# Reading the moving columns of every float32r matmul from two halves in turns

## The chip, the core and the metric

The kernel runs on one NeuronCore of a Trainium2 chip. A core has a matrix engine (TensorE, in the profile PE, its weight loads PEld), three engines for element-wise work (VectorE or DVE, ScalarE or ACT, GpSimd or POOL), a queue engine (SyncE or SP) and DMA engines. Operands lie in the on-chip memory SBUF, 128 partitions wide; matmuls write to the accumulators in PSUM, from which VectorE and ScalarE copy. The metric is the device time of one execution in microseconds.

## The reference

```python
# q, k, v: (4, 6080, 256); moe_w_in: (256, 2048); moe_w_out: (2048, 256)
qn = q / (np.linalg.norm(q, axis=1, keepdims=True) + 1e-06)
kn = k / (np.linalg.norm(k, axis=1, keepdims=True) + 1e-06)
s = kn.transpose(0, 2, 1) @ qn / tau          # 4 x 256 x 256
a = softmax(s, axis=-1)
x = (v @ a).reshape(24320, 256)
h = x @ w_in                                   # 24320 x 2048
g = np.where(h > 0.0, h, np.exp(np.minimum(h, 0.0)) - 1.0)
out = g @ w_out                                # 24320 x 256
```

The softmax is written in one word here; the reference subtracts the maximum and adds 1e-9 to the sum. The weights arrive as 64-bit floats and are converted on the chip.

## The kernel before

Attention is over channels, so for one batch a is a matrix of 256 x 256. The kernel multiplies it into the first weight matrix once per batch (wp = a times w_in, 256 x 2048), and what is left for each token is h = v wp, the ELU, and g w_out. Tokens are the columns: v comes in and the output goes out with channels first. The 24320 tokens are cut into 48 chunks, twelve per batch, eight of 512 and four of 496 columns (`chunk_sizes`). The 2048 hidden channels are cut into 16 tiles of 128, and one step (c, f) is one chunk and one such tile, 768 in all.

Nearly all products are in float32r, and each number of an operand is split into two float32r parts, hi and lo (`split`: ScalarE rounds to hi, VectorE subtracts). A product takes three matmuls: hi by hi, lo by hi, hi by lo. In a step `h_item` issues six into a PSUM tile ph (two contraction tiles of three, lines L323 to L325, moving operand vt, weights wp); `elu` makes e out of ph; `split_g` makes the pair g out of e; and three steps later (LAG = 3) `out_item` issues six into two PSUM tiles po (two output tiles of three, L361, L363, L365, moving operand g, weights wo). At a chunk's last step `store` copies the two po tiles to SBUF (L387) and sends them out. There are three po buffers and two are in use by a chunk.

In all of these the moving operand is a run of consecutive columns, such as `g[:, x, 0:n]`, 4 bytes a column, and each matmul writes its result's columns in the order in which it reads the moving ones. Two more kinds of float32r product run beside the steps: `gram_item` builds q-k products of the next batch from rows that were split in `split_rows` (L166 with 512 columns, in two runs of 256, and L169 with 256), and `wp_item` builds wp of the next batch (L283 to L285), scaled by the softmax's sums on its way out of PSUM (L289, L290). `softmax` reads the gram tiles (L229, L230). Batch 0 uses plain float32 for its gram (L446), its transposes and its wp (L281). Their moving operands are consecutive too.

The order of the engines' instructions is the program's order: a table of side jobs by step (`at`, `loose`, `fine`) sets where a conversion, a load or a gram matmul is issued among the steps.

After the last store twelve matmuls write a PSUM tile pd that nothing reads, the idle products: three plain ones (L696), three whose moving operand is one column repeated n times (L698), three on the same bytes seen as bf16 (L700), three on 64 of the 128 rows (L702).

Of the kernel before, what the change touches and what calls it, by code (L numbers as in the profile page):

```python
# [7 lines left out]
F32 = mybir.dt.float32  # L8
F32R = mybir.dt.float32r
U32 = mybir.dt.uint32  # L10
BF16 = mybir.dt.bfloat16
AF = mybir.ActivationFunctionType
ALU = mybir.AluOpType
AX = mybir.AxisListType
# [6 lines left out]
def chunk_sizes(n, most):  # L21

    unit = 16 if n % 16 == 0 else 2
    count = -(-n // most)
    low, more = divmod(n // unit, count)
    return [unit * (low + (x < more)) for x in range(count)]


@with_exitstack
def channel_attention_then_elu_ffn(ctx: ExitStack, tc, q, k, vT, tau, w_in, w_out, outT):  # L30
# [8 lines left out]
    nc = tc.nc  # L39
    B, N, C = q.shape  # L40
# [3 lines left out]
    P = 128  # L44
    KT = C // P
    FT = F // P
    DT = D // P
    CH = 512
    sizes = chunk_sizes(N, CH)
    NB = len(sizes)  # L50
    NCH = B * NB
# [7 lines left out]
    WB = 3  # L59
# [9 lines left out]
    ps = ctx.enter_context(tc.tile_pool(name="ps", bufs=4, space=bass.MemoryType.PSUM))  # L69
# [9 lines left out]
    wo = const.tile([P, FT, 2, D], F32R, name="wo")  # L79
# [78 lines left out]
    def gram_item(hl, gram, ct, first, last):  # L158

        pg = gram[ct]
        cs = slice(ct * P, ct * P + P)
        for r in range(2):
            yield nc.tensor.matmul(  # L166
                pg, hl[:, 0, 1, r, cs], hl[:, :, 0, r, :], start=(first and r == 0), stop=False
            )
            yield nc.tensor.matmul(  # L169
                pg[:, 0, :], hl[:, 1, 1, r, cs], hl[:, 0, 0, r, :], start=False, stop=(last and r == 1)  # L170
            )

    def keep_warm(n):
# [43 lines left out]
    def softmax(b, gram, pn, rk, nm):  # L217

        a = work.tile([P, KT, C], F32, tag="a", bufs=1, name=f"a_{b}")
        sm = tiny.tile([P, KT], F32, tag="sums", bufs=2, name="sums")
        for ct in range(KT):
            r = rk[:, ct : ct + 1]
            if b == 0:
                nc.vector.tensor_scalar(a[:, ct], gram[ct][:, 0, :], r, None, op0=ALU.mult)
                continue
            nc.scalar.copy(a[:, ct], gram[ct][:, 1, :])  # L229
            nc.vector.tensor_add(a[:, ct], gram[ct][:, 0, :], a[:, ct])  # L230
            if b == 1:
                nc.vector.tensor_add(a[:, ct], a[:, ct], early[:, ct])
            nc.vector.tensor_scalar(a[:, ct], a[:, ct], r, None, op0=ALU.mult)
        for ct in range(KT):
            nc.vector.tensor_mul(a[:, ct], a[:, ct], pn[:, 1, :])
            nc.vector.tensor_reduce(nm[:, ct : ct + 1], a[:, ct], axis=AX.X, op=ALU.max, negate=True)
            nc.scalar.activation(
                a[:, ct], a[:, ct], AF.Exp, bias=nm[:, ct : ct + 1], accum_out=sm[:, ct : ct + 1]
            )
        nc.vector.tensor_scalar(sm, sm, 1e-9, None, op0=ALU.add)  # L240
        done = nc.vector.reciprocal(sm, sm)
        return a, sm, done.ins
# [31 lines left out]
    def wp_item(aT, rs, wi, wp, ct, fq, part=0, parts=1):  # L274
        n = CH // parts
        pw = ps.tile([P, CH], F32, tag="w", bufs=WB, name="pw")[:, 0:n]
        cs = slice(ct * P, ct * P + P)
        ws = slice(part * n, part * n + n)
        for jt in range(KT):
            if wi.dtype == F32:  # L280
                nc.tensor.matmul(pw, aT[:, jt, cs], wi[:, jt, ws], start=(jt == 0), stop=(jt == KT - 1))  # L281
                continue
            nc.tensor.matmul(pw, aT[:, 0, jt, cs], wi[:, 0, jt, ws], start=(jt == 0), stop=False)  # L283
            nc.tensor.matmul(pw, aT[:, 0, jt, cs], wi[:, 1, jt, ws], start=False, stop=False)  # L284
            nc.tensor.matmul(pw, aT[:, 1, jt, cs], wi[:, 0, jt, ws], start=False, stop=(jt == KT - 1))  # L285
        f0 = fq * CH + part * n
        hi, lo = (wp[ct][:, x, f0 : f0 + n] for x in range(2))
        r = rs[:, ct : ct + 1]
        nc.scalar.activation(hi, pw, AF.Copy, scale=r)  # L289
        nc.vector.scalar_tensor_tensor(lo, pw, r, hi.bitcast(F32), op0=ALU.mult, op1=ALU.subtract)  # L290


    def span(c):

        b, x = divmod(c, NB)
        return b, b * N + sum(sizes[:x]), sizes[x]
# [17 lines left out]
    wps = {}  # L314

    def h_item(c, f, vt):
        b, _, n = span(c)
        wp = wps[b]
        ph = ps.tile([P, CH], F32, tag="w", bufs=WB, name="ph")
        fs = slice(f * P, f * P + P)  # L320
        for kt in range(KT):
            hi, lo = (vt[:, kt, x, 0:n] for x in range(2))
            nc.tensor.matmul(ph[:, 0:n], wp[kt][:, 0, fs], hi, start=(kt == 0), stop=False)  # L323
            nc.tensor.matmul(ph[:, 0:n], wp[kt][:, 0, fs], lo, start=False, stop=False)  # L324
            nc.tensor.matmul(ph[:, 0:n], wp[kt][:, 1, fs], hi, start=False, stop=(kt == KT - 1))  # L325
        return ph
# [22 lines left out]
    def first(c, f):  # L349
        return f == 0 or (c, f) in [(x, lo) for x, lo, _ in pieces]  # L350

    def last(c, f):
        return f == FT - 1 or (c, f) in [(x, hi - 1) for x, _, hi in pieces]

    def out_item(c, f, g, po, between):

        n = span(c)[2]
        hi, lo = (g[:, x, 0:n] for x in range(2))
        for dt in range(DT):
            o, ds = po[dt][:, 0:n], slice(dt * P, dt * P + P)  # L360
            nc.tensor.matmul(o, wo[:, f, 0, ds], hi, start=first(c, f), stop=False)  # L361
            next(between, None)
            nc.tensor.matmul(o, wo[:, f, 1, ds], hi, start=False, stop=False)  # L363
            next(between, None)
            nc.tensor.matmul(o, wo[:, f, 0, ds], lo, start=False, stop=last(c, f))  # L365
            next(between, None)

    def store(c, f, po):
        _, t0, n = span(c)
        ov = outT[:, t0 : t0 + n].rearrange("(k p) t -> p k t", p=P)  # L370
        if c < M:
            o = half[c]
        else:
            o = work.tile([P, DT, CH], F32, tag="o", bufs=1, name="o")
        for dt in range(DT):
            if c < M and (c, 0, f + 1) not in pieces:
                nc.vector.tensor_add(o[:, dt, 0:n], o[:, dt, 0:n], po[dt][:, 0:n])
            elif c == NCH - 1 and dt == DT - 1:

                m = n // 2  # L380
                nc.vector.tensor_copy(o[:, dt, 0:m], po[dt][:, 0:m])
                nc.scalar.copy(o[:, dt, m:n], po[dt][:, m:n])
                nc.sync.dma_start(ov[:, dt, 0:m], o[:, dt, 0:m])
                nc.scalar.dma_start(ov[:, dt, m:n], o[:, dt, m:n])
                continue
            else:
                nc.scalar.copy(o[:, dt, 0:n], po[dt][:, 0:n])  # L387
            if f == FT - 1:
                nc.sync.dma_start(ov[:, dt], o[:, dt, 0:n])

# [50 lines left out]
    wi64, wo64, vraw, vts = {}, {}, {}, {}  # L441
# [8 lines left out]
    with tc.manual_schedule(engines={nc.tensor.engine, nc.sync.engine}):  # L450
# [95 lines left out]
        for part in range(2):  # L546
            for ct in range(KT):
                wp_item(aT0, rs0, wf[0], wps[0], ct, 0, part, 2)
# [49 lines left out]
    for c in range(NCH - 1):  # L598
# [6 lines left out]
        x, y = ((1, 2), (4, 6), (17, 19))[c] if c < M - 1 else (c * FT + 9, c * FT + 12)  # L605
# [6 lines left out]
    for b in range(1, B):  # L612
# [18 lines left out]
        def gram(b, g, ct):  # L631
            g0 = first_group(b)
            yield from gram_item(state[b, "hl", g], state[b, "gram"], ct, g == g0, g == NG - 1)
# [10 lines left out]
        for g in range(g0, NG):  # L644
            x = s0 + length * (g - g0) // (NG - g0)
# [5 lines left out]
        x = s1 - FT - 6  # L651
# [12 lines left out]
    for i in range(len(steps) + LAG):  # L664
        if i < len(steps):
            c, f = steps[i]
# [5 lines left out]
        if j >= 0:  # L672
            c, f = steps[j]
# [12 lines left out]
                fn()  # L686

    c, n = NCH - 1, span(NCH - 1)[2]
    pd = ps.tile([P, CH], F32, tag="w", bufs=WB, name="pd")
    hi, lo = (vts[c][:, 0, x, 0:n] for x in range(2))
    wide, narrow = wps[B - 1][0][:, 0, 0:P], wo[:, 0, 0, 0:P]
    for _ in range(3):
        nc.tensor.matmul(pd[:, 0:n], wide, hi, start=True, stop=True)  # L696
    for w in (narrow, wide, narrow):
        nc.tensor.matmul(pd[:, 0:n], w, vts[c][:, 0, 0, 0:1].to_broadcast([P, n]), start=True, stop=True)  # L698
    for w, m in ((wide, hi), (narrow, lo), (wide, hi)):
        nc.tensor.matmul(pd[:, 0:n], w.bitcast(BF16)[:, 0:P], m.bitcast(BF16)[:, 0:n], start=True, stop=True)  # L700
    for w, m in ((wide, hi), (narrow, lo), (wide, hi)):
        nc.tensor.matmul(pd[:, 0:n], w[0 : P // 2], m[0 : P // 2], start=True, stop=True)  # L702


# [1 line left out]
_INS = ["q", "k", "v", "tau", "moe_w_in", "moe_w_out"]  # L706
_OUTS = [((256, 24320), "float32")]
# [26 lines left out]
```

## Time and profile before

| | us |
|---|---|
| median of 3 runs | 2292.24 |
| lowest and highest run | 2290.45, 2293.08 |
| the profiled execution | 2289.16 |
| its span, first to last instruction | 2287.4 |

| engine | busy us | share of the span | instructions |
|---|---|---|---|
| TensorE, matmuls | 2283.2 | 100% | 10244 |
| TensorE, weight loads | 1900.3 | 83% | 10244 |
| VectorE | 1533.4 | 67% | 2395 |
| ScalarE | 1480.7 | 65% | 2425 |

The granted TensorE clock is 1.000 over the whole span. A matmul's duration in the records reaches from its start to the modelled end of its last column and overlaps the next matmul; the distance from one start to the next is read from the timeline, where a row has the start in us, the duration in us, the engine, the line, the operation, output and inputs, and the shape. A row of a group has the line, engine, operation, output and inputs, shape and count, then the busy time in us and the mean in ns, then the engine's idle time before it. A row of waits has who waited for whom, the total in us, how many times, and the longest.

### The profile page before, as it was taken

The page shows a single profiled execution, that of the slowest core. Times are in us where ns is not written, and L with a number is a line of the kernel's source. Part 1 is how long each engine was busy: PE and PEld are TensorE (multiplying, and loading weights), DVE is VectorE, ACT ScalarE, POOL GpSimd, SP SyncE. Part 2 cuts the span into 40 slices and gives each one's busy share as a digit, 9 for nine tenths or more (in the row PEclk, how much of TensorE's full clock was granted, in tenths as well). Part 3 has the DMA queues.
Part 4 walks back from the last instruction along what each step waited for, and adds up shares of the span by engine and source line. Part 5 has one row for each costly group of instructions (what it writes and reads, how often), then busy time and mean ns, then how long its engine had stood idle before and what let it go on. Part 6 is the DMA issues. An engine that isn't in the chain of part 4 may idle for free.

```text
span 2287.4 us, 27142 instructions
## 1 busy us (share of the span) xinstructions
PE 2283.2 (100%) x10244; PEld 1900.3 (83%) x10244; DVE 1533.4 (67%) x2395; ACT 1480.7 (65%) x2425; POOL 3.2 (0%) x11
## 2 busy tenths in 40 slices
PE   9999999999999999999999999999999999999999
PEld 8778888888888888888888888888888888888888
DVE  6995766666666666666666667666666666666665
ACT  5876666666666666666666666666666666666665
POOL 0000000000000000000000000000000000000000
DMA  9220111110201111111111111121102000000000
GB/s 356 83 74 19 61 59 65 55 53 37 65 28 56 47 53 49 55 55 44 37 55 37 46 47 56 47 64 46 47 34 64 20 19 28 28 19 10 19 9 19
DMA packets 61092, 118.15 MB, mean 52 GB/s; under 512 B 6048, under 2 KB 15904, under 8 KB 60960
## 3 DMA queue, kind: packets, MB, share of 16 engines
q1 hardware_dynamic: 60816, 116.29, 15.0%
q8 instruction: 80, 1.31, 0.2%
q14 instruction: 52, 0.43, 0.1%
q10 hardware_dynamic: 144, 0.13, 0.0%
HBM read 89.39 MB, written 27.00 MB: 51 GB/s over the span
## 4 chain that ended last, share of the span: by engine, by line
PE 97%; DMA 1%; DVE 1%; ACT 0%; issue 0%; SPq 0%; DVEq 0%; ACTq 0%
PE ph L323 15%; PE po L365 15%; PE po L361 15%; PE po L363 15%; PE ph L325 15%; PE ph L324 15%; PE gram L166 3%; PE gram L169 1%; DMA room<-in_k_dram 1%; PE pw L281 1%; PE pw L284 0%; PE pw L285 0%; PE pw L283 0%; DVE acc L145 0%; DMA wi<-in_moe_w_in_dram 0%; DMA raw<-in_k_dram 0%
## 5 line engine op out<-in xcount | busy, mean ns | idle before, releaser
L82 ACT CAST g<-e 128x512 fp32r<-128x512 f32 (+1 forms) x768 | 472.4, 615 | 507.6 <-DVE e L340 275.2
L83 DVE TENSOR_TENSOR g<-e,g 128x512 fp32r<-128x512 f32 (+1 forms) x768 | 526.4, 685 | 349.4 <-ACT g L82 314.1
L361 PE MATMUL po<-g,wo 128*128 128x512 f32 (+1 forms) x1536 | 596.0, 388 | 0.3 <-ACT g L82 0.3
L365 PE MATMUL po<-g,wo 128*128 128x512 f32 (+1 forms) x1536 | 596.0, 388 | 0.0
L363 PE MATMUL po<-g,wo 128*128 128x512 f32 (+1 forms) x1536 | 595.4, 388 | 0.0
L323 PE MATMUL ph<-vt,wp 128*128 128x512 f32 (+1 forms) x1472 | 573.6, 390 | 0.0
L325 PE MATMUL ph<-vt,wp 128*128 128x512 f32 (+1 forms) x1472 | 570.7, 388 | 0.0
L324 PE MATMUL ph<-vt,wp 128*128 128x512 f32 (+1 forms) x1472 | 569.6, 387 | 0.0
L336 DVE SCALAR_TENSOR_TENSOR e<-e,ph 128x512 f32<-128x512 f32 (+1 forms) x416 | 283.6, 682 | 297.2 <-ACT e L335 296.4
L334 ACT ACTIVATE e<-ph 128x512 f32<-128x512 f32 (+1 forms) x416 | 247.1, 594 | 159.2 <-PE ph L325 155.7
L361 PEld LDWEIGHTS po<-g,wo 128*128 128x128 f32 x1536 | 288.4, 188 | 58.3 <-ACT g L82 0.7
L363 PEld LDWEIGHTS po<-g,wo 128*128 128x128 f32 x1536 | 288.4, 188 | 57.7
L365 PEld LDWEIGHTS po<-g,wo 128*128 128x128 f32 x1536 | 288.3, 188 | 52.3 <-DVE g L83 0.4
L323 PEld LDWEIGHTS ph<-vt,wp 128*128 128x128 f32 x1472 | 276.2, 188 | 56.6 <-PE po L365 0.6
L325 PEld LDWEIGHTS ph<-vt,wp 128*128 128x128 f32 x1472 | 276.3, 188 | 56.3
L324 PEld LDWEIGHTS ph<-vt,wp 128*128 128x128 f32 x1472 | 276.4, 188 | 56.0 <-issue 0.7
L335 ACT ACTIVATE e<-e 128x512 f32<-128x512 f32 (+1 forms) x416 | 261.2, 628 | 12.1
L338 ACT ACTIVATE e<-ph 128x512 f32<-128x512 f32 (+1 forms) x352 | 208.7, 593 | 79.2 <-PE ph L325 64.7
L340 DVE TENSOR_TENSOR e<-ph,e 128x512 f32<-128x512 f32 (+1 forms) x352 | 241.1, 685 | 10.7
L339 DVE TENSOR_SCALAR e<-e 128x512 f32<-128x512 f32 (+1 forms) x352 | 148.9, 423 | 49.7 <-ACT e L338 49.6
L145 DVE TENSOR_TENSOR acc<-acc,sq 128x1024 f32<-128x1024 f32 x84 | 102.6, 1221 | 12.1 <-ACT sq L144 11.4
L166 PE MATMUL gram<-qk 128*128 128x512 f32 x276 | 108.5, 393 | 0.0
(126 smaller groups left out, 1173.4 us busy)
## 6 DMA issues: line engine op xcount, KB each, us to landing
raw<-in_q_dram SPq DMA_DIRECT2D x73, 256.0 KB, 2.7
raw<-in_k_dram SPq DMA_DIRECT2D x73, 256.0 KB, 2.9
v<-in_v_dram SPq DMA_DIRECT2D x32, 512.0 KB, 3.4
out_dram<-o SPq DMA_DIRECT2D x56, 256.0 KB, 2.0
v<-in_v_dram SPq DMA_DIRECT2D x16, 496.0 KB, 3.5
out_dram<-o SPq DMA_DIRECT2D x31, 248.0 KB, 2.1
wraw<-w_scr SPq DMA_DIRECT2D x12, 512.0 KB, 3.1
room<-in_q_dram SPq DMA_DIRECT2D x16, 256.0 KB, 5.2
```

Of the source, the lines that this page charges most:

```text
L82: nc.scalar.copy(hi, src)
L83: nc.vector.tensor_sub(lo, src, hi.bitcast(F32))
L323: nc.tensor.matmul(ph[:, 0:n], wp[kt][:, 0, fs], hi, start=(kt == 0), stop=False)
L324: nc.tensor.matmul(ph[:, 0:n], wp[kt][:, 0, fs], lo, start=False, stop=False)
L325: nc.tensor.matmul(ph[:, 0:n], wp[kt][:, 1, fs], hi, start=False, stop=(kt == KT - 1))
L334: nc.scalar.activation(ev, pv, AF.Relu, scale=-1.0)
L335: x = nc.scalar.activation(ev, ev, AF.Exp, scale=-1.0)
L336: y = nc.vector.scalar_tensor_tensor(ev, ev, -1.0, pv, op0=ALU.add, op1=ALU.max)
L340: y = nc.vector.tensor_tensor(ev, pv, ev, op=ALU.max)
L361: nc.tensor.matmul(o, wo[:, f, 0, ds], hi, start=first(c, f), stop=False)
L363: nc.tensor.matmul(o, wo[:, f, 1, ds], hi, start=False, stop=False)
L365: nc.tensor.matmul(o, wo[:, f, 0, ds], lo, start=False, stop=last(c, f))
```

## The change

Four helpers give views of a run of columns. `in_turns` lists column 0, column n/2, column 1, column n/2 + 1 and so on. The others are used where a result is taken out of PSUM, so that its columns come back into their own order: `halves` with `halves_of_turns` after one product in turns, `quarters` with `quarters_of_turns` after two (the columns of ph, e and g are in turns after the first product, and g is read in turns again).

All float32r matmuls read their moving operand through `in_turns`. Number and order of the matmuls and their weights stay as they are. The element-wise work between ph and g is unchanged, in the changed column order. The idle products are left out.

```diff
+def in_turns(cols):
+    if len(cols.shape) == 3:
+        return cols.rearrange("p x (a b) -> p x b a", a=2)
+    return cols.rearrange("p (a b) -> p b a", a=2)
+
+def halves(cols):
+    return cols.rearrange("p (a b) -> p a b", a=2)
+
+def halves_of_turns(cols):
+    return cols.rearrange("p (b a) -> p a b", a=2)
+
+def quarters(cols):
+    return cols.rearrange("p (r s q) -> p r s q", r=2, s=2)
+
+def quarters_of_turns(cols):
+    return cols.rearrange("p (q r s) -> p r s q", r=2, s=2)
...
 # gram_item
-                pg, hl[:, 0, 1, r, cs], hl[:, :, 0, r, :], start=(first and r == 0), stop=False
+                pg,
+                hl[:, 0, 1, r, cs],
+                in_turns(hl[:, :, 0, r, :]),
...
-                pg[:, 0, :], hl[:, 1, 1, r, cs], hl[:, 0, 0, r, :], start=False, stop=(last and r == 1)
+                pg[:, 0, :],
+                hl[:, 1, 1, r, cs],
+                in_turns(hl[:, 0, 0, r, :]),
...
 # softmax
-            nc.scalar.copy(a[:, ct], gram[ct][:, 1, :])
-            nc.vector.tensor_add(a[:, ct], gram[ct][:, 0, :], a[:, ct])
+            row = halves(a[:, ct])
+            nc.scalar.copy(row, halves_of_turns(gram[ct][:, 1, :]))
+            nc.vector.tensor_add(row, halves_of_turns(gram[ct][:, 0, :]), row)
...
 # wp_item
-            nc.tensor.matmul(pw, aT[:, 0, jt, cs], wi[:, 0, jt, ws], start=(jt == 0), stop=False)
-            nc.tensor.matmul(pw, aT[:, 0, jt, cs], wi[:, 1, jt, ws], start=False, stop=False)
-            nc.tensor.matmul(pw, aT[:, 1, jt, cs], wi[:, 0, jt, ws], start=False, stop=(jt == KT - 1))
+            whi, wlo = (in_turns(wi[:, x, jt, ws]) for x in range(2))
+            nc.tensor.matmul(pw, aT[:, 0, jt, cs], whi, start=(jt == 0), stop=False)
+            nc.tensor.matmul(pw, aT[:, 0, jt, cs], wlo, start=False, stop=False)
+            nc.tensor.matmul(pw, aT[:, 1, jt, cs], whi, start=False, stop=(jt == KT - 1))
...
+        if wi.dtype != F32:
+            hi, lo, pw = halves(hi), halves(lo), halves_of_turns(pw)
...
 # h_item
-            hi, lo = (vt[:, kt, x, 0:n] for x in range(2))
+            hi, lo = (in_turns(vt[:, kt, x, 0:n]) for x in range(2))
...
 # out_item
-        hi, lo = (g[:, x, 0:n] for x in range(2))
+        hi, lo = (in_turns(g[:, x, 0:n]) for x in range(2))
...
 # store
+            y, x = quarters(o[:, dt, 0:n]), quarters_of_turns(po[dt][:, 0:n])
             if c < M and (c, 0, f + 1) not in pieces:
-                nc.vector.tensor_add(o[:, dt, 0:n], o[:, dt, 0:n], po[dt][:, 0:n])
+                nc.vector.tensor_add(y, y, x)
...
-                nc.vector.tensor_copy(o[:, dt, 0:m], po[dt][:, 0:m])
-                nc.scalar.copy(o[:, dt, m:n], po[dt][:, m:n])
+                nc.vector.tensor_copy(y[:, 0], x[:, 0])
+                nc.scalar.copy(y[:, 1], x[:, 1])
...
-                nc.scalar.copy(o[:, dt, 0:n], po[dt][:, 0:n])
+                nc.scalar.copy(y, x)
...
-    pd = ps.tile([P, CH], F32, tag="w", bufs=WB, name="pd")
...
-        nc.tensor.matmul(pd[:, 0:n], w[0 : P // 2], m[0 : P // 2], start=True, stop=True)
```

More of the change, by code (lines that the diff above doesn't have):

```diff
@@ L10 @@
 U32 = mybir.dt.uint32
-BF16 = mybir.dt.bfloat16
 AF = mybir.ActivationFunctionType
@@ L166, in gram_item @@
             yield nc.tensor.matmul(
-                pg, hl[:, 0, 1, r, cs], hl[:, :, 0, r, :], start=(first and r == 0), stop=False
+                pg,
+                hl[:, 0, 1, r, cs],
+                in_turns(hl[:, :, 0, r, :]),
+                start=(first and r == 0),
+                stop=False,
             )
             yield nc.tensor.matmul(
-                pg[:, 0, :], hl[:, 1, 1, r, cs], hl[:, 0, 0, r, :], start=False, stop=(last and r == 1)
+                pg[:, 0, :],
+                hl[:, 1, 1, r, cs],
+                in_turns(hl[:, 0, 0, r, :]),
+                start=False,
+                stop=(last and r == 1),
             )
@@ L686, in channel_attention_then_elu_ffn @@
                 fn()
-    c, n = NCH - 1, span(NCH - 1)[2]
-    pd = ps.tile([P, CH], F32, tag="w", bufs=WB, name="pd")
[L693 to L702, printed above, removed]
 _INS = ["q", "k", "v", "tau", "moe_w_in", "moe_w_out"]
```

## The prediction

> **What bounds the kernel now.** I read the page's first part, then the chain that ended last, then what TensorE waited for.
>
> ```profile
> span 2287.4 us, 27142 instructions
> PE 2283.2 (100%) x10244; PEld 1900.3 (83%) x10244; DVE 1533.4 (67%) x2395; ACT 1480.7 (65%) x2425; POOL 3.2 (0%) x11
> PE 97%; DMA 1%; DVE 1%; ACT 0%; issue 0%; SPq 0%; DVEq 0%; ACTq 0%
> ```
>
> ```profile
> PE pd L177 <- DVE ones L78: 1.1, 1, 1.1
> ...
> PE po L361 <- ACT g L82: 0.3, 1, 0.3
> ```
>
> TensorE is on 97% of the chain. The list of its waits has five entries; the largest and the last are shown, 1.1 us and 0.3 us, so nothing else holds it up worth the name. The other two engines stand a third idle. The time is therefore the number of matmuls times the distance from one start to the next, and a busy share can't tell that distance, since the 0.39 us of one matmul overlap the following one. So I counted in the groups of instructions, kept apart by form, and read distances from the timeline.
>
> ```profile
> L365 PE MATMUL po<-g,wo 128*128 128x512 f32 x1024 | 399.8, 391 | 0.0
> L323 PE MATMUL ph<-vt,wp 128*128 128x512 f32 x960 | 376.5, 392 | 0.0
> L323 PE MATMUL ph<-vt,wp 128*128 128x496 f32 x512 | 197.1, 385 | 0.0
> L166 PE MATMUL gram<-qk 128*128 128x512 f32 x276 | 108.5, 393 | 0.0
> L169 PE MATMUL gram<-qk 128*128 128x256 f32 x276 | 76.7, 278 | 0.0
> L323 PE MATMUL ph<-scr_r,wp 128*128 128x512 f32 x64 | 26.2, 409 | 0.0
> L285 PE MATMUL pw<-wi,aT 128*128 128x512 f32 x48 | 18.7, 390 | 0.0
> ```
>
> Six lines (L323, L324, L325, L361, L363, L365) carry 1024 matmuls of 512 columns each (960 + 64 for the first three) and 512 of 496. With 276 at L166 and 48 at each of L283 to L285 that makes 6144 + 276 + 144 = 6564 float32r matmuls of 512 columns, 3072 of 496 and 276 of 256.
>
> ```profile
> 169.01 0.39 PE L323 MATMUL ph<-vt,wp 128*128 128x512 f32 x1
> ...
> 177.17 0.39 PE L323 MATMUL ph<-vt,wp 128*128 128x512 f32 x1
> ```
>
> ```profile
> 2278.22 0.38 PE L361 MATMUL po<-g,wo 128*128 128x496 f32 x1
> ...
> 2283.28 0.38 PE L365 MATMUL po<-g,wo 128*128 128x496 f32 x1
> ```
>
> ```profile
> 814.49 0.28 PE L169 MATMUL gram<-qk 128*128 128x256 f32 x1
> 814.60 0.40 PE L365 MATMUL po<-g,wo 128*128 128x512 f32 x1
> ```
>
> Between the first two rows lie 36 steps: 8.16 / 36 = 0.2267 us for 512 columns. Between the next two lie 23: 5.06 / 23 = 0.2200 us for 496. The 256 columns take 0.11 us. The first two are 0.443 ns a column, and the third agrees within its last digit, so the distance goes with the columns and has next to no fixed part: 6564 x 0.2267 + 3072 x 0.2200 + 276 x 0.11 = 2194 us of the 2287.4.
>
> **The change, part by part.** The matmuls, their weights and their order stay. Only the order in which the moving columns are read differs: column j, then column j + n/2, which lies n x 2 bytes on (1 KB at 512). No row of this trace has such a read, so its price is bounded. What the trace has is one set of reads that are cheaper than consecutive ones, and one that takes twice as long.
>
> ```profile
> 2284.16 0.37 PE L698 MATMUL pd<-vt,wo 128*128 128x496 f32 x1
> ...
> 2284.80 0.38 PE L700 MATMUL pd<-vt,wp 128*128 128x496 bf16 x1
> ...
> 2285.23 0.37 PE L700 MATMUL pd<-vt,wp 128*128 128x496 bf16 x1
> ```
>
> ```profile
> 57.26 3.45 PE pw L281 x16
> 92.03 1.72 PE pw L281 x4
> ```
>
> L698 reads one column over and over: three starts in 0.64 us, 0.2133 each, against 0.2200 for 496 different columns. L700 reads half as many bytes: two in 0.43 us, 0.215. The weights at L698 are loaded as float32, as for any other matmul. So what makes 0.2200 out of 0.213 is the fetching of moving columns: at 4 bytes a column the read path is already the slower party, by 3%, with the easiest addresses there are. The second fence, from the chain in order of time, is the plain float32 product: 1.72 / 4 = 0.430 us for 512 columns and 3.45 / 16 = 0.2156 for 256, both at half the column rate.
>
> Lower end of the price: the new order removes the 3%. Upper end: every distance doubles, because two consecutive columns no longer come out of neighbouring addresses and each needs a fetch of its own. I take the second kind, at the distance of the nearest row in which the array takes a column every other beat, 0.430 us. The reason is the row before: a path that falls behind with neighbouring addresses has nothing to spare for scattered ones. The terms:
> - 512 columns: 6564 x (0.430 - 0.2267) = 1334 us
> - 496 columns: 3072 x (0.430 x 496/512 - 0.2200) = 604 us
> - 256 columns: 276 x (0.2156 - 0.11) = 29 us
>
> Together +1967 us. With doubled distances instead it would be the 2194 us themselves.
>
> The Trainium skill bears on this in Advanced Engine Details and Errata, section SBUF Cachelines: the memory is read in lines of 16 bytes, at least two hits on a line are needed to absorb its latency, and a different line on every access is penalised. It gives no price. Here consecutive reading has four float32 columns on a line, reading in turns has one, so by that rule the time goes up, and by the measured distances alone (order of addresses free) it would stay at 2292; no run so far shows a read of one column per line.
>
> The order of the columns is undone in four places, which costs the other engines something. wp is written through a column view (24 pairs at L289 and L290, one for every six of the 144), a softmax row likewise (6 pairs), and the output copy reads PSUM with a step of four columns and writes quarters.
>
> ```profile
> L335 ACT ACTIVATE e<-e 128x512 f32<-128x512 f32 x288 | 182.1, 633 | 8.3
> ...
> L95 ACT ACTIVATE cv<-wi 128x512 f32<-128x512 f32 x8 | 5.4, 673 | 0.7 <-DVE wf L107 0.6
> ```
>
> ```profile
> 2244.76 1.23 ACT L387 COPY o<-po 128x496 f32<-128x496 f32 x2
> ...
> 2247.20 0.38 PE L361 MATMUL po<-g,wo 128*128 128x496 f32 x1
> ```
>
> L95 reads every second word and takes 673 ns against 633 for a consecutive read of that size: 40 ns dearer. That, or at most as much again as the copy itself (0.6 us), is the price of one output copy. By the loops there are 95 (48 chunks of two, less the last half chunk) and 14 additions at L377. The cover is a chunk's end: two copies run from 2244.76 to 2245.99, and of the three po buffers the one freed first is wanted again at 2247.20. Behind the copies on ScalarE stands the next rounding of g, whose product comes two steps (5 us) later. Doubled copies would end at 2247.2 for both, the first at 2246.0, still in time. I put all four places at nothing; with slower matmuls the cover grows. Without cover it would be 95 x 0.6 = 57 us.
>
> The idle products at the end stand beside the last stores:
>
> ```profile
> 2284.55 0.38 ACTq L384 DMA_DIRECT2D out_dram<-o  x1
> ...
> 2286.08 0.39 PE L702 MATMUL pd<-vt,wp 64*128 64x496 f32 x1
> ```
>
> ```profile
> out_dram<-o ACTq DMA_DIRECT2D x1, 124.0 KB, 1.8
> ```
>
> The last store lands at 2284.55 + 1.8 = 2286.4, the last idle product ends at 2286.5. Taking them away gains 0.1 us, and the strided reads of the two last half copies (L381, L382) may take back 0.2 to 0.4 us. I put both at nothing.
>
> Sum: 2287.4 + 1967 = 4254 us of span. The profiled execution took 2289.16 us, 1.8 more than its span, and the median of the runs, 2292.24, lies 3.1 above that. So 4259 us; with doubled distances 4486.
>
> **The rivals.**
> - **Faster, 2225 us.** The 3% is not a limit of the path but a pause at some boundary of consecutive addresses; with two streams in turns each pause falls beside the other stream's data. It decides if two stretches of memory can be kept open at once. For it: distances of consecutive reads are 3% above those of one repeated column. Against it: it takes a buffer for two places, of which no row tells. Price: (0.2133 - 0.2200) x 3072 = -21, the same scaled to 512 columns x 6564 = -45, and -1 for the 256: -67 us. By the Trainium skill's TensorE: Matmul & The Clock Gate, section Back-to-back issue gap, warm matmuls follow each other at N / 2.4 + 2.5 ns, 215.8 at 512 columns where this trace has 226.7; if the pause went entirely, that estimate would give about -105 us, 2187.
> - **No change, 2292 us.** The columns are fetched one by one, whatever their addresses, and the 3% belongs to delivering new data at all, which L698 and L700 do less of. For it: the distance is strictly proportional to the columns. It is also what comes out if the pauses are merely shared between two streams.
> - **Somewhat slower, about 2680 us.** A scattered read costs TensorE what it costs ScalarE at L95, 40 ns per 512 columns: 6564 x 0.040 + 3072 x 0.039 + 276 x 0.02 = 388 us. Against it: that read still has neighbours 8 bytes apart, ours are 1 KB apart.
> - **Much slower, over 4600 us.** Each column waits for a whole fetch without overlap. No row prices it.
>
> **How the numbers follow.** About one column per two beats (own range 4100 to 4600): 0.58. Somewhat slower: 0.06. Much slower: 0.03. No change: 0.16. Faster: 0.17. A measurement of this kernel tells about 0.2% (4.6 us) from no change. So slower 0.58 + 0.06 + 0.03 = 0.67, same 0.16, faster 0.17. The predicted time is the likeliest's, 4259. A range for 8 in 10 has to take in no change beside it: 2285 to 4600 leaves out the faster case and the much slower one, 0.20.
>
> **What the profile of the changed kernel would show.** In the likeliest case the start-to-start distance at L323 and L361 (old numbers) is 0.41 to 0.46 us in every stage; the plain float32 stretches (to 57 us, and L281) keep their length; the clock stays 1.00; VectorE and ScalarE fall to some 36% and wait for TensorE. Output copies of 0.6 to 1.2 us with no wait of TensorE for them show the copies' step right. Distances of 0.22 to 0.23 make the prediction wrong altogether, and the price was then that of the repeated column or none. New waits of L361 for the output copy would show that their cover was misjudged.

## The result, and the profile after

The changed kernel takes 2180.76 us (four runs, 2180.24 to 2182.71) against 2291.59 before: a ratio of 0.952, interval 0.9505 to 0.9534. It is 111 us faster; the prediction said 4259 us, and its range began at 2285. The profiled execution took 2182.71 us, with a span of 2180.9.

The page of the changed kernel, the same three lines as before:

```profile
span 2180.9 us, 27141 instructions
PE 2169.1 (99%) x10232; PEld 1913.4 (88%) x10232; DVE 1519.3 (70%) x2395; ACT 1466.6 (67%) x2425; POOL 3.1 (0%) x11
PE 95%; DVE 2%; DMA 1%; ACT 1%; issue 0%; SPq 0%; DVEq 0%; ACTq 0%
```

TensorE is still the bound. The groups show twelve matmuls fewer and hardly a wait that is new (the largest at an output product is 2.1 us in all, below), so the matmuls themselves must stand closer. The timeline of the changed kernel says how close (L360 is the old L323, L398 the old L361):

```profile
2060.37 0.37 PE L360 MATMUL ph<-vt,wp 128*128 128x496 f32 x1
...
2100.53 0.37 PE L360 MATMUL ph<-vt,wp 128*128 128x496 f32 x1
```

```profile
399.90 0.38 PE L360 MATMUL ph<-vt,wp 128*128 128x512 f32 x1
...
403.14 0.38 PE L398 MATMUL po<-g,wo 128*128 128x512 f32 x1
```

Between the first two lie 16 steps of twelve matmuls: 40.16 / 192 = 0.2092 us for 496 columns, against 0.2200. Between the other two lie 15: 0.216 for 512, against 0.2267. Summed over all starts, each of the six lines of the steps gave back 16 to 19 us (103 together), the gram 6, wp 2; the start, where the plain float32 gram waits for its loads, took some 4 more. That is the whole difference of the spans, 106.5 us.

The output copy, before (L387) and after (L425), the waits of TensorE for it, and the end of the changed kernel:

```profile
L387 ACT COPY o<-po 128x512 f32<-128x512 f32 x56 | 32.0, 588 | 5.0 <-PE po L365 3.1
```

```profile
L425 ACT COPY o<-po 128x512 f32<-128x512 f32 x56 | 31.9, 587 | 3.9 <-PE po L402 2.7
```

```profile
PE po L398 <- DVE scr L415: 2.1, 2, 1.6
...
PE po L398 <- ACT g L107: 0.3, 1, 0.3
```

Reading PSUM with a step of four columns and writing quarters costs ScalarE nothing: 587 ns against 588.

### The profile page after: what moved, and what is told of

Its sections match the earlier page's. It is cut to its first block, busy times and chain, and to the rows that moved or that the text cites. A ratio compares the mean times of both kernels' runs of the same rounds, so it can differ in the third digit from the quotient of the medians.

```text
span 2180.9 us, 27141 instructions
## 1 busy us (share of the span) xinstructions
PE 2169.1 (99%) x10232; PEld 1913.4 (88%) x10232; DVE 1519.3 (70%) x2395; ACT 1466.6 (67%) x2425; POOL 3.1 (0%) x11
## 4 chain that ended last, share of the span: by engine, by line
PE 95%; DVE 2%; DMA 1%; ACT 1%; issue 0%; SPq 0%; DVEq 0%; ACTq 0%
PE po L398 15%; PE po L402 15%; PE po L400 15%; PE ph L360 15%; PE ph L362 15%; PE ph L361 15%; PE gram L191 3%; PE gram L198 1%; DVE acc L170 1%; DMA raw<-in_k_dram 1%; PE pw L319 0%; PE pw L320 0%; PE pw L318 0%; PE pw L315 0%; DMA room<-in_k_dram 0%
## 5 line engine op out<-in xcount | busy, mean ns | idle before, releaser
L398 PE MATMUL po<-g,wo 128*128 128x512 f32 (+1 forms) x1536 | 580.5, 378 | 2.5 <-DVE scr L415 2.1
L402 PE MATMUL po<-g,wo 128*128 128x512 f32 (+1 forms) x1536 | 579.5, 377 | 0.1
L400 PE MATMUL po<-g,wo 128*128 128x512 f32 (+1 forms) x1536 | 579.6, 377 | 0.0
L360 PE MATMUL ph<-vt,wp 128*128 128x512 f32 (+1 forms) x1472 | 557.1, 379 | 0.4 <-DVE e L373 0.4
L361 PE MATMUL ph<-vt,wp 128*128 128x512 f32 (+1 forms) x1472 | 555.0, 377 | 0.0
L362 PE MATMUL ph<-vt,wp 128*128 128x512 f32 (+1 forms) x1472 | 554.9, 377 | 0.0
L398 PEld LDWEIGHTS po<-g,wo 128*128 128x128 f32 x1536 | 290.8, 189 | 41.8 <-DVE scr L415 3.6
L360 PEld LDWEIGHTS ph<-vt,wp 128*128 128x128 f32 x1472 | 278.6, 189 | 38.0 <-DVE e L373 1.0
L361 PEld LDWEIGHTS ph<-vt,wp 128*128 128x128 f32 x1472 | 278.7, 189 | 36.4 <-issue 0.7
```

## Experiments: one part at a time

**Without the idle products.** The kernel before, without its last twelve matmuls.

```diff
-    c, n = NCH - 1, span(NCH - 1)[2]
-    pd = ps.tile([P, CH], F32, tag="w", bufs=WB, name="pd")
...
-        nc.tensor.matmul(pd[:, 0:n], w[0 : P // 2], m[0 : P // 2], start=True, stop=True)
```

> The kernel before without its twelve idle products, nothing else changed. All theories: 0.1 us less or no difference (ratio 0.999 to 1.001), since the last store lands when the last idle product ends. If they had held back anything more, some 2 us.

Measured 2291.26 us, ratio 0.9999 (0.9989 to 1.0009). They stood beside the last store, and this part of the change is worth nothing.

**Only v, gram and wp in turns.** g is read consecutively again.

```diff
-        hi, lo = (in_turns(g[:, x, 0:n]) for x in range(2))
+        hi, lo = (g[:, x, 0:n] for x in range(2))
...
-            y, x = quarters(o[:, dt, 0:n]), quarters_of_turns(po[dt][:, 0:n])
+            y, x = halves(o[:, dt, 0:n]), halves_of_turns(po[dt][:, 0:n])
```

> The changed kernel with g read consecutively again in the output product (the output copy then undoes one turn of columns instead of two); v, the gram and wp stay in turns. If each matmul is paid for by itself: 3072 of 512 columns and 1536 of 496 go back to 0.2267 and 0.2200 us, so 2180.8 + 3072 x 0.0110 + 1536 x 0.0108 = 2231 us (ratio to before 0.974), and the trace shows 0.2267 at the output product beside 0.2157 at the hidden one. If what counts is the mixture (the pause of a consecutive matmul is owed to the one before or behind it), the two lines share the extra time and the total lies nearer to one end, 2181 or 2291.

Measured 2238.54 us, ratio 0.9767 (0.9753 to 0.9782). Its timeline:

```profile
2100.47 0.37 PE L360 MATMUL ph<-vt,wp 128*128 128x496 f32 x1
...
2101.72 0.38 PE L398 MATMUL po<-g,wo 128*128 128x496 f32 x1
...
2103.06 0.37 PE L360 MATMUL ph<-vt,wp 128*128 128x496 f32 x1
```

Six matmuls in turns take 1.25 us (0.208 each), the six consecutive ones behind them 1.34 (0.223). So each matmul pays for its own reading, and the gain is had line by line. The total is 7 us above the expected one, because consecutive matmuls between others come out at 0.223 here and not at 0.2200. Such stretches stand in the kernel before too; why a disturbed series of consecutive reads stays a few ns slower is not settled.

## Experiments: what a read costs

**A first ladder of reads.** The next kernel is the changed one with 27 groups of 24 equal matmuls behind it, 512 columns and 128 weight columns unless said, the moving operand taken from the tile wo. Each ladder is a single execution. One group as an example:

```diff
+    flat = wo.rearrange('p f x d -> p (f x d)')
+    mv = flat[:, 0:512].rearrange('p (o a b) -> p o b a', a=2, b=4)
+    for _ in range(24):
+        nc.tensor.matmul(pd[0:128, 0:512], W, mv, start=True, stop=True)  # d4
```

> The changed kernel with 27 groups of 24 equal float32r matmuls behind its last product (some 0.15 ms longer for that); each group's start-to-start distance is the result. Reference groups: 512 consecutive columns 0.2267 us (544 beats of 2.4 GHz, 32 more than columns), in turns from halves 0.2157 (518). Theory A, boundary: a consecutive read pauses one beat at each 64 bytes, that is 16 columns, and a second stream covers the pause. Then 256 columns take 272 beats (0.1133 us), the number of weight columns does not matter (0.2267 with 64 and 32 of them), constant data in distinct columns take 0.2267 as well, and the distance of the two streams matters: turns within 4, 8 or 16 columns stay in one piece of 64 bytes and are no better than consecutive, turns over 32 columns and more are. Theory B, weight load: the fetches of 128 float32 weights (512 bytes, 32 lines of 16 bytes) take 32 beats from a moving read that has no beat to spare. Then 256 consecutive columns take 288 beats (0.120 us), 64 weight columns give 528 beats (0.220 us) and 32 give 520 (0.2167), and weights with a step of four columns, one to a line, cost more still. Theory C, shape of the walk: a read in an inner loop of two elements is fed differently from one long run. Then every turn, even within 4 columns, gives 0.2157, and evens-then-odds, step 4 and step 16 stay at 0.2267. What the prediction held, that a column without a neighbour costs a second beat, would show at step 4 and step 16: 0.43.

The timeline merges a group into one row, so a group's cost is the next row's start less its own, divided by 24. A beat is used below as a unit, 1/2.4 ns: one more consecutive column costs about as much, (5.47 - 2.88) / 24 / 256 = 0.42 ns in the first rows. In order: consecutive; in turns from halves; 256 consecutive (then 256 in turns, left out); 64 weight columns; 32; in turns with 64; turns inside four columns (0 2 1 3); inside eight (0 4 1 5); inside sixteen.

```profile
2176.44 5.63 PE L736 MATMUL pd<-wo,wp 128*128 128x512 f32 x24
2181.91 5.34 PE L739 MATMUL pd<-wo,wp 128*128 128x512 f32 x24
2187.09 3.04 PE L742 MATMUL pd<-wo,wp 128*128 128x256 f32 x24
...
2192.65 5.68 PE L748 MATMUL pd<-wo,wp 128*64 128x512 f32 x24
2198.16 5.72 PE L751 MATMUL pd<-wo,wp 128*32 128x512 f32 x24
2203.72 5.34 PE L754 MATMUL pd<-wo,wp 128*64 128x512 f32 x24
2208.90 5.63 PE L757 MATMUL pd<-wo,wp 128*128 128x512 f32 x24
2214.37 5.34 PE L760 MATMUL pd<-wo,wp 128*128 128x512 f32 x24
2219.55 5.34 PE L763 MATMUL pd<-wo,wp 128*128 128x512 f32 x24
```

Consecutive 5.47 / 24 = 0.228 us, in turns 5.18 / 24 = 0.216. The 256 consecutive columns take 2.88 / 24 = 0.120 us (288 beats), as theory B alone forecast, but fewer weight columns do not help (0.230, 0.232), so B falls. Turns inside four columns are no better than consecutive (0.228), inside eight as good as from halves (0.216). That contradicts theory A, which wanted them apart by 64 bytes, and theory C, which asked for no distance at all. The border lies between turns inside four and inside eight columns, where a half is two columns or four, 8 bytes or 16. Further down the same kernel: runs of two, four, eight and sixteen columns taken in turns from the halves; evens then odds; every fourth column; every sixteenth; four places in turns; one column repeated; constant data in distinct columns; the next group's start.

```profile
2240.27 8.32 PE L775 MATMUL pd<-wo,wp 128*128 128x512 f32 x24
2248.42 6.18 PE L778 MATMUL pd<-wo,wp 128*128 128x512 f32 x24
2254.43 6.00 PE L781 MATMUL pd<-wo,wp 128*128 128x512 f32 x24
2260.28 5.92 PE L784 MATMUL pd<-wo,wp 128*128 128x512 f32 x24
2266.03 11.03 PE L787 MATMUL pd<-wo,wp 128*128 128x512 f32 x24
2276.89 11.25 PE L790 MATMUL pd<-wo,wp 128*128 128x512 f32 x24
2287.96 10.58 PE L793 MATMUL pd<-wo,wp 128*128 128x512 f32 x24
2298.36 6.97 PE L796 MATMUL pd<-wo,wp 128*128 128x512 f32 x24
2305.16 5.41 PE L799 MATMUL pd<-wo,wp 128*128 128x512 f32 x24
2310.41 5.65 PE L802 MATMUL pd<-same,wp 128*128 128x512 f32 x24
2315.90 5.84 PE L805 MATMUL pd<-wo,wp 128*128 128x512 f32 x24
```

The doubling that was forecast exists: evens then odds take 10.86 / 24 = 0.4525 us, every fourth column 0.461, every sixteenth 0.433. It is no worse with one column in 64 bytes than with two in 16. These fit one picture, theory P: the columns go in pairs, the first members form a stream and the second members another, and each stream pays for its visits to pieces of 16 bytes. Consecutive, a stream takes columns 0, 2, 4, 6: two at a visit. In turns it takes 0, 1, 2, 3: four at a visit. Evens then odds, it takes 0, 4, 8: one. A rival, S, has the gain come from two places at once.

Some groups do not fit a count of visits. Runs of two, four, eight and sixteen columns in turns took 815, 601, 585 and 575 beats, where 4.25 beats a visit give 1088 and three times 544; four places in turns took 680 (6.80 / 24 us) in place of 1088. Consecutive columns from column 1 (L805, up to the next group's start at 2321.58) took 568, some 20 more than from column 0. What a stream pays when it jumps between two places, and what a shifted start adds, is open.

**A second ladder, to tell P from S.**

```diff
+    mv = view(flat, 0, [[1, 256], [0, 2]])
...
+    mv = view(flat, 0, [[2, 256], [512, 2]])
```

> The changed kernel with 27 other groups of 24 matmuls behind it. Theory P, pair streams: a float32r matmul takes its columns in pairs, the first members of the pairs form one stream and the second members another, each stream goes to memory in pieces of 16 bytes (four columns), and one visit to a piece costs 4.25 beats of 2.4 GHz (544 / 128 for consecutive columns, where a stream takes two columns at a visit; 1088 / 256 for evens-then-odds, one at a visit; with four at a visit 64 x 4.25 = 272 beats hide behind 512). Rival S, two places: a pair is read faster when its members come from two pieces at once, whatever the step inside a stream. Expected in beats at 512 columns: each column twice (0 0, 1 1, 2 2), and 0 1, 1 2, 2 3, and 0 2, 1 3, 2 4: P 518 all three, since each stream advances by one column; S 544 for the first, between for the others. Halves in turns with step 2: P 544, S 518. With step 3: P 192 visits, 816; S 518. With step 4: P 1088, S 518. Three of four, in turns (510 columns): P 516. In turns from column 1, and with the second half one column on: both 518. The steps in n: P takes 1.0625 n for consecutive columns (544, 476, 408, 340, 272) where nothing else bounds, against n + 32 (544, 480, 416, 352, 288) if the extra were a fixed cost of a matmul; in turns n + 6 for both. bf16 has no forecast: if its columns go in pairs too, step 4 (8 bytes, so 16 within a stream) costs 1088 and step 2 544; if they go four at a time, step 2 does already.

Each column twice; 0 1, 1 2, 2 3; 0 2, 1 3, 2 4; halves in turns with step 2, with step 3, with step 4; three of four columns; and the start of the next group:

```profile
2216.88 5.35 PE L767 MATMUL pd<-wo,wp 128*128 128x512 f32 x24
2222.06 5.34 PE L770 MATMUL pd<-wo,wp 128*128 128x512 f32 x24
2227.24 5.36 PE L773 MATMUL pd<-wo,wp 128*128 128x512 f32 x24
2232.44 5.63 PE L776 MATMUL pd<-wo,wp 128*128 128x512 f32 x24
2237.90 8.32 PE L779 MATMUL pd<-wo,wp 128*128 128x512 f32 x24
2246.05 11.00 PE L782 MATMUL pd<-wo,wp 128*128 128x512 f32 x24
2256.87 5.35 PE L785 MATMUL pd<-wo,wp 128*128 128x510 f32 x24
2262.06 5.36 PE L788 MATMUL pd<-wo,wp 128*128 128x512 f32 x24
```

The first two have no second place and take 0.216 (518 beats); the third takes 520. Halves with step 2 have two places and take 0.2275 (546), as consecutive reading does; step 3 gives 0.3396 (815, forecast 816), step 4 0.4508 (1082, forecast 1088), three of four 0.2163 (519, forecast 516). P holds at each, and S falls.

In the sizes P held less well: consecutive reads of 512, 448, 384, 320 and 256 columns took 547, 487, 417, 352 and 288 beats, where visits alone give 544, 476, 408, 340, 272. The other forecast on record, a fixed cost of 32 beats a matmul (544, 480, 416, 352, 288), comes nearer in the last four. bf16 behaved differently from float32r, consecutive 518 beats, step 2 542, step 4 1082, step 8 2160, which is one stream without pairs at some 4.25 beats a visit. Some 4 us into the step 8 group the granted TensorE clock fell from 1.00 to 0.50, but its matmuls took 0.900 us each before and after that, so the time of a visit did not follow this clock. (The two groups behind it ran mostly at the lower clock and are left out.)

**A third ladder, on the open points.**

```diff
+    mv = view(flat, 0, [[2, 384]])
...
+    mv = view(flatb, 0, [[1, 256], [256, 2]])
```

> The changed kernel with 21 groups behind it (24 matmuls each, 8 of plain float32). Open after the first two: whether the extra beats of a stream that takes two columns at a visit go with the visits (0.25 beat on each four) or are some 32 a matmul, since 512, 384, 320 and 256 consecutive columns took 547, 416, 351 and 288 beats. Read from halves with step 2 (512, 384, 256 columns): by visits 544, 408, 272; fixed 544, 416, 288. Evens only, step 2 of one run (512, 384, 256): by visits 1088, 816, 544; if 64 are fixed 1088, 832, 576. Step 4 with 512 and 256: by visits 1088 (1107 was measured) and 544. Step 2 with 64 weight columns: 1088 if the weights have no part, 1056 or less if they have. For bf16 a single stream, with no pairs, fits what was measured (4.25 beats for each piece of 16 bytes: 544, 1088 and 2176 at steps 2, 4 and 8). Then from column 1: 518; runs of 4 in turns between halves: 64 visits in each half, 128 in turns, 544 or less; step 3: 192 visits, 816; halves in turns: 512 visits, over 1300. If bf16 were read in pairs like float32r, halves in turns would take 518. Plain float32 (two records a matmul, 428 ns each at 512 columns): consecutive and in turns alike 0.428, since a column every other beat leaves a visit eight beats.

Step 2 with 512, 384 and 256 columns; step 4 follows:

```profile
2188.51 10.99 PE L749 MATMUL pd<-wo,wp 128*128 128x512 f32 x24
2199.32 8.34 PE L752 MATMUL pd<-wo,wp 128*128 128x384 f32 x24
2207.47 5.62 PE L755 MATMUL pd<-wo,wp 128*128 128x256 f32 x24
2212.92 11.25 PE L758 MATMUL pd<-wo,wp 128*128 128x512 f32 x24
```

That is 1081, 815 and 545 beats where visits give 1088, 816 and 544: where the visits are clearly the limit, the cost goes with them, some 4.25 beats each, and nothing is fixed. (Step 4 is a little dearer: 1107 and 560 beats for 512 and 256 columns, 4.3 and 4.4 a visit.) Halves with step 2 gave 551, 419 and 287 beats for 512, 384 and 256 columns, against 544, 408, 272 by visits and 544, 416, 288 with a fixed cost: the same surplus at small sizes as consecutive reads. So at two columns a visit a matmul pays 3 to 16 beats beyond its visits, and these runs do not tell a cost by visits from a fixed one there; why is open. Step 2 with 64 weight columns took 1081, so ordinary weight loads have no part. (In the first ladder, weights with one column to 16 bytes slowed both orders to 0.235 and 0.238 us, as theory B had it; no kernel here has such weights.)

bf16 from halves in turns, bf16 runs of four in turns, bf16 with step 3, and plain float32, consecutive, in turns, with step 2 and with step 4 (eight matmuls each, which leave 16 records):

```profile
2257.62 11.79 PE L776 MATMUL pd<-wo,wp 128*128 128x512 bf16 x24
2269.25 5.60 PE L779 MATMUL pd<-wo,wp 128*128 128x512 bf16 x24
2274.69 8.32 PE L782 MATMUL pd<-wo,wp 128*128 128x512 bf16 x24
2282.84 7.03 PE L785 MATMUL pd<-wo,wp 128*128 128x512 f32 x16
2289.71 8.80 PE L788 MATMUL pd<-wo,wp 128*128 128x512 f32 x16
2298.35 7.36 PE L791 MATMUL pd<-wo,wp 128*128 128x512 f32 x16
2305.55 14.56 PE L794 MATMUL pd<-wo,wp 128*128 128x512 f32 x16
```

In turns, bf16 takes 11.63 / 24 = 0.485 us where it takes 0.216 consecutively, and plain float32 0.540 a record where it takes 0.429. For plain float32 the expectation (alike) missed, and bf16's 1163 beats are fewer than the 1300 expected; bf16 runs of four (5.44 / 24, 544 beats) and step 3 (816) came out as expected. Neither looks paired: read in pairs, bf16 would have taken 518 beats in turns, and plain float32 would cost as much with step 4 as with step 2, but a record takes 0.450 us with step 2 and about 0.90 with step 4. So reading in turns only makes more visits for them. A slowdown like the forecast one is what these groups let expect of this change in a bf16 kernel; no such kernel was run.

## Experiments: the whole kernel again

**Turns inside eight columns, and inside four**, for v and g.

```diff
-    return cols.rearrange("p (a b) -> p b a", a=2)
+    return cols.rearrange("p (o a b) -> p o b a", a=2, b=4)   # b=2 for four
```

> The changed kernel with the turns taken inside each block of eight columns (0 4 1 5 2 6 3 7) in place of the halves of the whole, for v and g; gram and wp as in the changed kernel. P: each stream still takes four columns at a visit, so 0.2157 us at the hidden and the output product and the changed kernel's time, 2181 us (ratio to before 0.952). A theory in which the two halves have to lie far apart: up to 2291.

> The same inside blocks of four columns (0 2 1 3). Two such turns give the old order again, so the output copy is the one of before. P: a stream takes two columns at a visit, as in consecutive reading, so 0.227 us at both products and the time of before less the gram's and wp's share (420 matmuls of 512 columns by 0.011 us and 276 of 256 by about 0.006): 2285 us (ratio 0.997). S, or a gain from the two-column inner loop as such: 2181.

Eight: 2177.99 us, ratio 0.9505 (0.9489 to 0.9521). Four: 2287.30 us, ratio 0.9983 (0.9973 to 0.9992). The hidden product of the first and of the second, 180 and 192 matmuls apart:

```profile
1901.05 0.38 PE L368 MATMUL ph<-vt,wp 128*128 128x512 f32 x1
...
1939.90 0.38 PE L368 MATMUL ph<-vt,wp 128*128 128x512 f32 x1
```

```profile
2060.39 0.39 PE L368 MATMUL ph<-vt,wp 128*128 128x512 f32 x1
...
2103.91 0.39 PE L368 MATMUL ph<-vt,wp 128*128 128x512 f32 x1
```

0.2158 against 0.2267 us. Both kernels read v and g out of order, in a loop of the same kind and with as many instructions. Blocks of four need no undoing at the output copy, since two such turns give the old order, but undoing was free above (587 ns against 588). What is left is how many columns a stream finds in a piece of 16 bytes, and that is worth 109 us.

**The two good versions on one chip.**

> The changed kernel once more, on the chip of the next one, for comparison: ratio to before 0.952.

> Turns inside blocks of eight columns, as before, beside the changed kernel on one chip. If only the columns taken at a visit count, the two are equal (difference under 0.2%, some 4 us). If the nearness of the two members is worth something, this one is faster by the 3 us that lay between their medians on different chips.

The changed kernel took 2181.05 us (ratio 0.9519, 0.9506 to 0.9532), turns inside eight 2177.38 (0.9505, 0.9492 to 0.9518). The 3.7 us between them are 0.17%, inside the forecast for equal, but the same side was ahead by 2.8 us on different chips, so the medians leave a small gain possible. The traces show none at the matmuls: in both the median distance of the hidden and output products is 0.216 us at 512 columns and 0.209 at 496. The listed waits of TensorE add up to 7.8 us in the profile of the changed kernel and 3.8 in the other, 4.0 of the 4.8 us between these two spans (2179.2 and 2174.4). In the earlier profile of turns inside eight they add up to 6.6, so they differ from run to run; whether the order has any part in them is not settled. Both beat the kernel before.

## Why the prediction was wrong

- **What bounds the kernel** was right: matmuls times their distance. The distances 0.2267 and 0.2200 were right too, and so was the thought that a part of each is owed to the fetching of moving columns, which the repeated column betrayed (0.007 us by that row, 0.011 as measured). "Next to no fixed part" does not hold: consecutive columns in a long series took about 32 beats more than their number at 256 columns as at 512 (288 and 547 beats). That was no large term, since 276 matmuls of 256 columns are all it concerned.
- **The step that failed** is the choice of the upper end: "because two consecutive columns no longer come out of neighbouring addresses and each needs a fetch of its own". By theory P, whose forecasts for steps 2, 3 and 4 came true, neighbours in the order of reading are not fetched together: in float32r the members of a pair belong to two streams, and the change turned each stream from two columns per 16 bytes to four. Instead of 0.430 us the runs showed 0.2158 for 512 columns (0.2092 for 496), so in place of +1967 us the spans show -106.5. The sentence that a path which "falls behind with neighbouring addresses has nothing to spare for scattered ones" took the new order to be more scattered than the old, when for each stream it is denser. The anchor row, plain float32 at 0.430 us, said nothing about scattered reads; it is the time of one record, and a plain float32 matmul leaves two (16 for eight matmuls in the third ladder), so "half the column rate" misread it.
- **The rival that came true, "Faster"**, had 0.17. Its direction and the removal of the pause were right; its reason, two stretches of memory kept open at once, was wrong: a second place is neither needed (each column twice, 518 beats) nor enough (halves with step 2, 546). Its price of 67 us was mis-sized: the repeated column at 0.2133 was no floor, since alone in a long series of 512 it takes 5.25 / 24 = 0.219, while columns in turns take 0.2158. The 67 became 111.
- **What the skill said.** The estimate by the Trainium skill's TensorE: Matmul & The Clock Gate, section Back-to-back issue gap, was 2187 us; its 215.8 ns at 512 columns is what the changed kernel has (0.2158), so the trace agrees. The Trainium skill's Advanced Engine Details and Errata, section SBUF Cachelines, was applied to the wrong sequence. Counted per stream, its 16 bytes agree with the border between turns inside four and inside eight columns; its two hits do not quite: two columns at a visit still cost float32r 5% (0.2267 against 0.2158), and the measurement decides.
- **The side terms** held: undoing the order was free (587 ns a copy, 2.1 us of new waits for the additions at L415), and so were the idle products (0.9999).

## What to carry to other kernels

A float32r matmul of 512 consecutive columns took 5% longer here than one in turns (0.2267 against 0.2158 us), where TensorE was the bound throughout. In such a kernel arrange the moving columns so that the first and the second members of the pairs each walk through memory by one column, in turns of two blocks of at least four columns, and undo the order where the result leaves PSUM, which cost nothing here. Do not carry it to bf16 or plain float32, where the test groups in turns took 2.2 and 1.26 times as long. And before calling an access pattern scattered, find out which columns the hardware fetches together: a dozen groups of test matmuls behind the last product of a kernel answer that in one run.

## What the runs showed of the hardware

- A visit of one stream to a piece of 16 bytes takes some 4.25 beats (1081 / 256 = 4.22 with float32r columns two apart, 815 / 192 = 4.24 from halves with step 3, 1107 / 256 = 4.32 four apart). It is hidden with three or four columns at a visit (519 and 518 beats).
- The time of a visit did not follow the granted TensorE clock: bf16 columns 16 bytes apart took 0.900 us a matmul at 1.00 and at 0.50.
- Streams that go back and forth between two places pay less than that for each visit: four places in turns, where each stream alternates between two, took 6.80 / 24 = 0.283 us, 680 beats for 256 visits of a stream, or 2.7 each. Runs of two columns in turns took 815 / 256 = 3.2. Something of the last piece may be kept; no run here settles what, and longer runs in turns cost more than their visits, not less.
- Constant data in distinct columns take 0.2288 us, like any others: the pause hangs on addresses, not on values.
